# Softmax attention on one core: splitting the first V load, moving one transpose, and recutting the last V load

## The chip, the cores and the metric

The kernel runs on one core of a Trainium2 chip. The metric is the device time of one execution in microseconds. A core has a matrix engine (TensorE, PE in the profile, with weight loads listed apart as PEld), a vector engine (VectorE, DVE), a scalar engine (ScalarE, ACT), GpSimd (POOL), and SyncE (SP), which in this kernel only issues DMA transfers. Sixteen DMA engines move data between the chip's memory and the core's on-chip memory.

## The reference

Attention without a mask, for 8 x 16 = 128 heads, each with 16 queries, 2048 keys and values, and a head width of 256, all in bf16:

```python
B, H, Sq, Skv, Dh = 8, 16, 16, 2048, 256
scores = jnp.einsum('bhqd,bhkd->bhqk', q, k) * scale      # scale = Dh ** -0.5
attn   = softmax(scores, axis=-1)
out    = jnp.einsum('bhqk,bhkd->bhqd', attn, v)
```

K and V are 134 MB each and every byte of them is used once; Q and the output are 1 MB each.

## The kernel before

Eight heads form a block, so there are G = 16 blocks, and the last has the number 15. In a block, 8 heads x 16 queries fill the 128 partitions. K of a block comes in two units (e = 0 and 1) of 4 MB; a unit holds 128 partitions x 64 tokens x 256 values (T = 64). V of a block is 128 partitions x 128 tokens x 256 values, 8 MB.

On-chip there are four slots of 4 MB in the tensor SL, numbered VA, VB, KA and KB. V of a block fills VA and VB, the two K units of a block fill KA and KB. Only K of block 0 is an exception: it is loaded into VA and VB, so that K of block 1 can be loaded into KA and KB at once.

What a block goes through:

- VectorE transposes K in place, in two halves (h = 0 and 1) per unit: the helper kt(e, h, slot), line 195. Each transpose counts up c_kt.
- TensorE multiplies K by the queries into four banks of S_ps (lines 309 and 310, called from qk; for block 0 from a loop of its own). It works unit by unit and half by half, each half waiting for its transpose. c_qk counts 4 per finished unit, so 8 per block.
- VectorE takes the maximum over S_ps (line 218), ScalarE the exponential into P_sb (line 292), VectorE transposes the weights into PTa and PTb (lines 229 and 231) and makes the reciprocal of the sum (line 234).
- ScalarE (line 277) and VectorE (lines 202 and 204) copy the weights into PTz, the layout that TensorE reads. Half of these copies must wait until TensorE has used up the weights of the block before.
- TensorE multiplies the weights by V in 128 steps, one per token (the function pv, line 331). It counts up c_pv once per 16 tokens, so 8 per block. c_pv starts at 8, so that the counts of block b reach 8 * b + 16 at its end.
- ScalarE scales the result by the reciprocal (line 271) and issues the store of the block's output.

TensorE's order is: scores of block 0; then for r = 1 to 16 the scores of block r (if there is one) and after them the V product of block r - 1. Before some V products a few spare matmuls into X_ps run (line 310 also); the rounds at both ends have none.

SyncE issues all loads, in the order of its program (on_sync, lines 128 to 156), all on one queue: Q, the two K units of block 0, the two of block 1, V of block 0; then for each further block its two K units and V of the block before. A load is preceded by a wait until its slot has been used up: a K unit of block j waits for c_qk (the scores of the same unit of block j - 1), V of a block waits for c_pv (the V product of the block before). V of block 0 goes into VA and VB, where K of block 0 was, and so waits for c_qk 8: the scores of both units of block 0. The last two V loads (blocks 14 and 15) are cut into pieces by tokens (PIECES, lines 104 and 105); a piece starts when the product of the block before has passed its tokens, and the product of its own block waits for each piece, on a semaphore for every piece but the first.

VectorE's program (on_vector) before its loop over blocks transposes the four halves of K of block 0 and the first half of the first unit of block 1, line 213. Inside the loop, behind the maximum, a branch taken in block 0 alone transposes the second half of that unit (line 222), and another one, behind the reciprocal, both halves of the second unit (line 238).

All orders are written out by hand; there is no scheduler. The functions:

Of the kernel before, what the change touches and what calls it, by code (L numbers as in the profile page):

```python
# [14 lines left out]
T = 64  # L15
SPARE = 5
VA, VB, KA, KB = 0, 1, 2, 3
C = 16


def bass_standalone__softmax_full_bidir__sampling_kernel(
# [11 lines left out]
    last = G - 1  # L33
# [5 lines left out]
    vb = v.rearrange("b h s d -> (b h s) d").rearrange("(g p t) d -> g p t d", p=128, t=2 * T)  # L39
# [3 lines left out]
    with ExitStack() as es:  # L43
# [22 lines left out]
        def sem(name):  # L66
            return ec(nc.semaphore(name))
# [3 lines left out]
        s_k = [sem("s_ka"), sem("s_kb")]  # L71
        s_kl = [sem("s_kla"), sem("s_klb")]
        s_v = sem("s_v")
        s_st = sem("s_st")
        s_fin = sem("s_fin")
        c_pool = sem("c_pool")
# [4 lines left out]
        c_qk = sem("c_qk")  # L81
# [8 lines left out]
        c_pv = sem("c_pv")  # L90
# [11 lines left out]


        PIECES = {last - 1: [(0, 56), (56, 40), (96, 32)],
                  last: [(0, 37), (37, 27), (64, 19), (83, 14), (97, 10), (107, 7), (114, 5), (119, 4), (123, 3), (126, 2)]}

        s_p = {w: {a: sem("s_p%d_%d" % (w, a)) for a, n in PIECES[w][1:]} for w in PIECES}
        VW = SL[:, VA:VB + 1, :, :].rearrange("p a t d -> p (a t) d")


        def weights(e, r, x):
            rows = slice(32 * r, 32 * r + (32 if x else 16))
            m = 32 * r + 16 * x
            if e == x:
                src = PTa[rows, :, 16 * x:16 * x + 16]
            else:
                src = PTb[rows, e:e + T, 16 * x:16 * x + 16]
            return PTz[rows, e, :, m:m + 16], src, mk[rows, :]

        def qx(Q, a):  # L120

            return (QTu[32 * a:32 * a + 32, 8 * Q:8 * Q + 8, :, :].rearrange("p u c y -> p c u y"),
                    QXu[32 * Q:32 * Q + 32, a, :, :, :].rearrange("p u c y -> p c u y"))

        def load_k(eng, g, e, slot, t0, n, s):
            eng.dma_start(SL[:, slot, t0:t0 + n, :], ku[2 * g + e, :, t0:t0 + n, :]).then_inc(s, 16)

        def on_sync(eng):
            def load_v(w, a, n):

                if isinstance(w, int) and w == 0:
                    eng.wait_ge(c_qk, 8)
                else:
                    eng.wait_ge(c_pv, 8 * w + (a + n + C - 1) // C)
                eng.dma_start(VW[:, a:a + n, :], vb[w, :, a:a + n, :]).then_inc(s_p[w][a] if a else s_v, 16)  # L135

            eng.dma_start(QX, qh).then_inc(s_q, 16)  # L137
            for g, s0, s in ((0, VA, s_k0), (1, KA, s_k)):
                for e in range(2):
                    load_k(eng, g, e, s0 + e, 0, T, s[e])  # L140
            load_v(0, 0, 2 * T)
            with nc.Fori(2, last, engines=[SP]) as j:
                for e in range(2):
                    eng.wait_ge(c_qk, 8 * j + 4 * e - 4)
                    load_k(eng, j, e, KA + e, 0, T, s_k[e])
                load_v(j - 1, 0, 2 * T)
            for e in range(2):
                eng.wait_ge(c_qk, 8 * last + 4 * e - 4)
                load_k(eng, last, e, KA + e, 0, T // 2, s_k[e])
                load_k(eng, last, e, KA + e, T // 2, T // 2, s_kl[e])  # L150
            for w in PIECES:
                for a, n in PIECES[w]:
                    load_v(w, a, n)
            eng.wait_ge(c_ev, G + 1)
            eng.dma_start(oh[last], O_fin[:]).then_inc(s_fin, 16)
            eng.wait_ge(s_fin, 16)
# [19 lines left out]
        def on_vector(eng):  # L176
            eng.memset(QW[:].rearrange("p e m x -> p (e m x)").bitcast(F32), 0.0).then_inc(c_qt, 1)
            eng.memset(mk[:], 1.0).then_inc(c_mk, 1)
            eng.memset(P_sb[:, 0:16], 0.0).then_inc(c_mk, 1)
            eng.memset(P_sb[:, 2064:2080], 0.0).then_inc(c_mk, 1)  # L180
            eng.wait_ge(c_mk, 3)
            for r in range(4):
                eng.memset(mk[32 * r:32 * r + 16, :], 0.0).then_inc(c_mk, 1)
            eng.wait_ge(s_q, 16)
            qf = QX.bitcast(F32)
            eng.transpose(qf, qf).then_inc(c_qt, 1)  # L186
            eng.wait_ge(c_qt, 2)
            for a in range(4):
                eng.tensor_copy(*qx(0, a)).then_inc(c_qt, 1)
            fa = PTa[:].rearrange("p t x -> p (t x)")  # L190
            fb = PTb[:].rearrange("p t x -> p (t x)")

            def kt(e, h, slot):
                x = SLf[:, slot, 32 * h:32 * h + 32, :].rearrange("p t i -> p (t i)")
                eng.transpose(x, x).then_inc(c_kt, 1)  # L195

            def copies(e, rs):
                for r in rs:
                    for x in range(2):
                        dst, src, m = weights(e, r, x)  # L200
                        if x:
                            ins = eng.tensor_scalar(out=dst, in0=src, scalar1=m, scalar2=None, op0=ALU.mult)  # L202
                        else:
                            ins = eng.tensor_copy(dst, src)  # L204
                        ins.then_inc(c_cd, 1)

            for e in range(2):
                eng.wait_ge(s_k0[e], 16)
                for h in range(2):
                    kt(e, h, VA + e)  # L210

            eng.wait_ge(s_k[0], 16)
            kt(0, 0, KA)
            eng.wait_ge(c_pool, 2)
            eng.wait_ge(c_mk, 7)
            with nc.Fori(0, G, engines=[DVE]) as g:  # L216
                eng.wait_ge(c_qk, 8 * g + 8)
                eng.tensor_reduce(out=negm[:], in_=S_ps[:].rearrange("p c n -> p (c n)"),  # L218
                                  axis=AX.X, op=ALU.max, negate=True).then_inc(c_mx, 1)
                gg = eng.to_reg(g)  # L220
                with eng.If_eq(gg, 0):
                    kt(0, 1, KA)
                for h in range(2):
                    eng.wait_ge(c_ex[h], g + 1)
                    if h == 0:

                        eng.wait_ge(c_cp, 10 * g + 1)
                    n = 1024 + 32 * h
                    eng.transpose(fa[:, 1024 * h:1024 * h + 1024],  # L229
                                  P_sb[:, 16 + 1024 * h:16 + 1024 * h + 1024]).then_inc(c_pt, 1)  # L230
                    eng.transpose(fb[:, 1024 * h:1024 * h + n], P_sb[:, 1024 * h:1024 * h + n]).then_inc(c_pt, 1)  # L231
                eng.tensor_reduce(out=ltot[:], in_=lsum[:], axis=AX.X, op=ALU.add).then_inc(c_ri, 1)
                eng.wait_ge(c_ri, 2 * g + 3)
                eng.reciprocal(rinv[:, bass.ds(g + 2, 1)], ltot[:]).then_inc(c_ri, 1)
                with eng.If_eq(gg, 0):
                    eng.wait_ge(s_k[1], 16)
                    for h in range(2):
                        kt(1, h, KB)

                mid = eng.to_reg(((g + 15) & 16) + ((g + 1) & 16))  # L240
                with eng.If_eq(mid, 16):
                    eng.wait_ge(s_k[0], 16 * g + 16)
                    kt(0, 0, KA)
                eng.wait_ge(c_pv, 8 * g + 4)
                copies(0, (2, 3))
                with eng.If_eq(mid, 16):
                    eng.wait_ge(s_kl[0], ((g + 2) & 16) + 1)
                    kt(0, 1, KA)
                eng.wait_ge(c_pv, 8 * g + 8)
                copies(1, (3,))  # L250
                with eng.If_eq(mid, 16):
                    eng.wait_ge(s_k[1], 16 * g + 16)
                    kt(1, 0, KB)
                    eng.wait_ge(s_kl[1], ((g + 2) & 16) + 1)
                    kt(1, 1, KB)
# [49 lines left out]
        def on_tensor(eng):  # L305
# [16 lines left out]
            def pv(lim):  # L322

                for t in range(2 * T):
                    if t == T:
                        eng.wait_ge(c_cp, 10 * r + 1)
                        eng.wait_ge(c_cd, 6 * r)
                    for w in s_p:
                        if t in s_p[w]:
                            eng.wait_ge(s_p[w][t], lim[w])  # L330
                    ins = eng.matmul(O_ps[:, 0:D], PTz[:, t // T, t % T, :], VW[:, t, :],  # L331
                                     start=(t == 0), stop=(t == 2 * T - 1))
                    if t % C == C - 1:
                        ins.then_inc(c_pv, 1)
# [18 lines left out]
            with nc.Fori(1, G + 1, engines=[PE]) as r:  # L353
# [20 lines left out]
                pv(lim)  # L374

        on_sync(nc.sync)
        on_gpsimd(nc.gpsimd)
        on_vector(nc.vector)
# [30 lines left out]
```

## Time and profile before

| what | value |
|---|---|
| median of 3 runs | 635.7 us (635.33, 635.70, 636.56) |
| the profiled execution | 636.47 us, span 635.2 us |
| mean granted clock of TensorE | 0.976 |
| TensorE matmul busy | 536.8 us, 85% |
| VectorE busy | 444.2 us, 70% |
| ScalarE busy | 241.8 us, 38% |
| read from memory | 269.48 MB |
| mean rate over the span | 426 GB/s |
| K unit transposes (line 195) | 64, 4434 ns each |
| V product steps (line 331) | 2048, 274 ns each, overlapping |

The span runs from the first to the last recorded instruction or transfer; the execution's time is a little longer. Times in the profile count from the start of the span, in us. PE, PEld, DVE, ACT and POOL are the engines named above; a q behind an engine's name is its instruction queue. L195 is line 195 of the kernel. A row of the chain gives start, length and what the time went to. A row of a timeline gives start, length, engine, line, operation, destination and source, the count, and in square brackets how long the engine had been idle before and what ended that. A row of windows gives the stretch, its length, the busy time of PE, PEld, DVE, ACT and POOL with the number of instructions, the granted TensorE clock (1.00 is full speed), the busy share of the DMA engines and the rate in GB/s; in it a DMA record is counted where it starts, with its whole length, so that short windows can show shares above 1.

### The profile page before, as it was taken

Reading aid. Unit: us, or ns where it says so; the run is one execution under the profiler, and the core shown is the slowest. Engines: PE = TensorE matmul, PEld = TensorE weight load, DVE = VectorE, ACT = ScalarE, POOL = GpSimd, SP = SyncE. Lnnn points to the kernel's source line nnn. Section 1 sums busy time; section 2 is a strip of 40 time slices with the busy share of each in tenths; the row PEclk is TensorE's granted clock in tenths of the full one; section 3 lists DMA queues with packets and bytes.
Section 4 is the critical chain, followed back from the end, with each engine's and each line's share of the span. In section 5 each row is a group of like instructions: output and inputs, shape, how many; then the busy total and the mean of one; then the engine's idle time right before and its main releaser. Section 6 shows DMA issues by size and latency. Waiting matters only on the chain.

```text
span 635.2 us, 8052 instructions
## 1 busy us (share of the span) xinstructions
PE 536.8 (85%) x3271; PEld 274.5 (43%) x2561; DVE 444.2 (70%) x285; ACT 241.8 (38%) x309; POOL 21.5 (3%) x18
## 2 busy tenths in 40 slices
PE   1658979899798898978989789898888988889988
PEld 0112724517244182542725336263352724518377
DVE  5979795766948658496575966759567594769740
ACT  1025542623426233352424425244262342623552
POOL 7600000000000000000000000000000000000000
PEclk9998999999999998999989999898999989999999
DMA  8999999999999999999999999999999999999997
GB/s 365 450 435 400 427 435 427 434 424 431 459 404 457 406 440 440 426 451 416 448 430 420 445 417 444 449 407 458 405 457 412 428 442 431 451 406 429 429 423 280
DMA packets 11234, 270.56 MB, mean 426 GB/s; under 512 B 1248, under 2 KB 3552, under 8 KB 4192
## 3 DMA queue, kind: packets, MB, share of 16 engines
q1 hardware_dynamic: 9072, 269.55, 98.6%
q10 hardware_dynamic: 2160, 0.98, 0.5%
q8 instruction: 1, 0.02, 0.0%
q14 instruction: 1, 0.01, 0.0%
HBM read 269.48 MB, written 1.05 MB: 426 GB/s over the span
## 4 chain that ended last, share of the span: by engine, by line
DMA 53%; PE 37%; DVE 5%; issue 4%; SPq 0%; DVEq 0%; ACT 0%
DMA SL<-in_v_dram 48%; PE O_ps L331 32%; DMA SL<-in_k_dram 5%; DVE SL L195 4%; PE S_ps L309 3%; PE S_ps L310 2%; DVE PTa L229 0%; DVE PTb L231 0%; DVE PTz L202 0%; DVE PTz L204 0%; SPq L135 0%; ACT O_fin L271 0%; SPq L137 0%; DVEq L240 0%; DVEq L216 0%
## 5 line engine op out<-in xcount | busy, mean ns | idle before, releaser
L195 DVE STREAM_TRANSPOSE SL<-SL 128x4096 f32<-128x4096 f32 x64 | 282.4, 4434 | 80.5 <-DMA SL<-in_k_dram 79.7
L309 PE MATMUL S_ps<-SL,QW 128*128 128x512 bf16 (+1 forms) x512 | 206.2, 403 | 70.4 <-DVE SL L195 60.9
L331 PEld LDWEIGHTS O_ps<-SL,PTz 128*128 128x128 bf16 x2048 | 200.1, 98 | 102.2 <-DMA SL<-in_v_dram 77.6
L331 PE MATMUL O_ps<-SL,PTz 128*128 128x256 bf16 x2048 | 228.0, 274 | 12.6 <-DMA SL<-in_v_dram 12.6
L310 PE MATMUL S_ps<-SL,QW 128*128 128x512 bf16 (+1 forms) x512 | 204.7, 400 | 0.0
L309 PEld LDWEIGHTS S_ps<-SL,QW 128*128 128x128 bf16 (+1 forms) x512 | 74.3, 145 | 246.3 <-issue 154.4
L263 ACT ACTIVATE QW<-QT 32x256 bf16 x64 | 26.9, 420 | 201.8 <-PE S_ps L310 200.7
L218 DVE TENSOR_REDUCE negm<-S_ps 128x1 f32<-128x2048 f32 x16 | 36.7, 2292 | 58.8 <-PE S_ps L310 58.8
L277 ACT ACTIVATE PTz<-PTa 16x1024 bf16<-16x1024 bf16 x32 | 33.8, 1056 | 114.4 <-PE O_ps L331 99.7
L310 PE MATMUL X_ps<-QT,QW 128*128 128x512 bf16 x195 | 52.7, 379 | 3.4
L277 ACT ACTIVATE PTz<-PTb 16x1024 bf16<-16x1024 bf16 x48 | 50.6, 1055 | 10.9 <-ACT O_fin L271 10.1
L277 ACT ACTIVATE PTz<-PTa,mk 32x1024 bf16<-32x1024 bf16 x48 | 54.3, 1130 | 0.0
L229 DVE STREAM_TRANSPOSE PTa<-P_sb 128x1024 bf16<-128x1024 bf16 x32 | 39.1, 1222 | 20.5 <-ACT P_sb L292 20.5
L231 DVE STREAM_TRANSPOSE PTb<-P_sb 128x1024 bf16<-128x1024 bf16 (+1 forms) x32 | 39.0, 1218 | 0.0
L292 ACT ACTIVATE P_sb<-S_ps,negm 128x1024 bf16<-128x1024 f32 x32 | 35.3, 1109 | 5.4 <-DVE negm L218 5.4
L277 ACT ACTIVATE PTz<-PTb,mk 32x1024 bf16<-32x1024 bf16 x32 | 36.2, 1132 | 0.0
L271 ACT ACTIVATE O_fin<-O_ps,rinv 128x256 bf16<-128x256 f32 x16 | 7.6, 474 | 52.5 <-PE O_ps L331 52.5
L202 DVE TENSOR_SCALAR PTz<-PTb,mk 32x1024 bf16<-32x1024 bf16 x32 | 15.2, 476 | 0.0
L204 DVE COPY PTz<-PTa 16x1024 bf16<-16x1024 bf16 x32 | 13.5, 422 | 1.6 <-PE O_ps L331 0.6
L169 POOL COPY QT<-PTz 32x1024 bf16<-32x1024 bf16 x12 | 14.3, 1193 | 3.1 <-DVE PTz L186 2.4
L204 DVE COPY PTz<-PTb 16x1024 bf16<-16x1024 bf16 x16 | 6.8, 424 | 3.4 <-PE O_ps L331 3.0
L309 PE MATMUL S_ps<-PTz 128*128 128x512 bf16 x1 | 0.6, 609 | 9.8 <-ACT QW L263 9.8
(21 smaller groups left out, 38.8 us busy)
## 6 DMA issues: line engine op xcount, KB each, us to landing
SL<-in_k_dram SPq DMA_DIRECT2D x30, 4096.0 KB, 24.3
SL<-in_k_dram SPq DMA_DIRECT2D x4, 2048.0 KB, 22.0
SL<-in_v_dram SPq DMA_DIRECT2D x1, 3584.0 KB, 21.0
SL<-in_v_dram SPq DMA_DIRECT2D x1, 2560.0 KB, 23.6
SL<-in_v_dram SPq DMA_DIRECT2D x1, 2368.0 KB, 10.6
SL<-in_v_dram SPq DMA_DIRECT2D x1, 2048.0 KB, 25.0
SL<-in_v_dram SPq DMA_DIRECT2D x1, 1728.0 KB, 13.1
SL<-in_v_dram SPq DMA_DIRECT2D x1, 1216.0 KB, 12.6
```

Source lines behind the costliest of these rows:

```text
L195: eng.transpose(x, x).then_inc(c_kt, 1)
L202: ins = eng.tensor_scalar(out=dst, in0=src, scalar1=m, scalar2=None, op0=ALU.mult)
L204: ins = eng.tensor_copy(dst, src)
L218: eng.tensor_reduce(out=negm[:], in_=S_ps[:].rearrange("p c n -> p (c n)"), axis=AX.X, op=ALU.max, negate=True).then_inc(c_mx, 1)
L229: eng.transpose(fa[:, 1024 * h:1024 * h + 1024], P_sb[:, 16 + 1024 * h:16 + 1024 * h + 1024]).then_inc(c_pt, 1)
L231: eng.transpose(fb[:, 1024 * h:1024 * h + n], P_sb[:, 1024 * h:1024 * h + n]).then_inc(c_pt, 1)
L263: eng.activation(dv, src(a), ACTF.Copy, scale=scale).then_inc(c_qw, 1)
L277: eng.activation(dst, src, ACTF.Copy, scale=m if x else 1.0).then_inc(c_cp, 1)
L292: eng.activation(P_sb[:, 16 + 1024 * h:16 + 1024 * h + 1024], sv, ACTF.Exp, bias=negm[:], scale=1.0, accum_out=lsum[:, h:h + 1]).then_inc( ...
L309: return eng.matmul(dst, w, x, start=start, stop=stop, skip_group_check=not check)
L310: return eng.add_instruction(mybir.InstMatmult(name=nc.get_next_instruction_name(), engine=PE, start_tensor_calc=start, stop_tensor_calc=stop,
L331: ins = eng.matmul(O_ps[:, 0:D], PTz[:, t // T, t % T, :], VW[:, t, :], start=(t == 0), stop=(t == 2 * T - 1))
```

## The change

Three edits, in three places.

1. V of block 0 is loaded in two halves of 64 tokens. The first half goes into VA and waits only for the first unit's scores of block 0 (c_qk 4); the second goes into VB and waits for c_qk 8 as before. The second half has a semaphore of its own, s_v0, and the V product waits for it at token 64 (in every block; after block 0 it is passed already).
2. Both halves of the first unit of block 1 are transposed ahead of VectorE's loop. The branch behind the maximum is gone.
3. V of the last block comes in nine pieces of 30, 25, 20, 16, 12, 10, 7, 5 and 3 tokens instead of ten of 37, 27, 19, 14, 10, 7, 5, 4, 3 and 2.

```diff
+        s_v0 = sem("s_v0")
...
-                  last: [(0, 37), (37, 27), (64, 19), (83, 14), (97, 10), (107, 7), (114, 5), (119, 4), (123, 3), (126, 2)]}
+                  last: [(0, 30), (30, 25), (55, 20), (75, 16), (91, 12), (103, 10), (113, 7), (120, 5), (125, 3)]}
...
             def load_v(w, a, n):
-                if isinstance(w, int) and w == 0:
-                    eng.wait_ge(c_qk, 8)
-                else:
-                    eng.wait_ge(c_pv, 8 * w + (a + n + C - 1) // C)
+                eng.wait_ge(c_pv, 8 * w + (a + n + C - 1) // C)
                 eng.dma_start(VW[:, a:a + n, :], vb[w, :, a:a + n, :]).then_inc(s_p[w][a] if a else s_v, 16)
...
-            load_v(0, 0, 2 * T)
+            for e in range(2):
+                eng.wait_ge(c_qk, 4 * e + 4)
+                eng.dma_start(VW[:, T * e:T * e + T, :], vb[0, :, T * e:T * e + T, :]).then_inc(s_v0 if e else s_v, 16)
...
             eng.wait_ge(s_k[0], 16)
-            kt(0, 0, KA)
+            for h in range(2):
+                kt(0, h, KA)
             eng.wait_ge(c_pool, 2)
             eng.wait_ge(c_mk, 7)
             with nc.Fori(0, G, engines=[DVE]) as g:
...
                 gg = eng.to_reg(g)
-                with eng.If_eq(gg, 0):
-                    kt(0, 1, KA)
...
                 for t in range(2 * T):
                     if t == T:
+                        eng.wait_ge(s_v0, 16)
                         eng.wait_ge(c_cp, 10 * r + 1)
                         eng.wait_ge(c_cd, 6 * r)
```

## The prediction

> **What bounds the kernel now.** I read the page first (busy shares, slices, the chain by engine), then the chain in order of time, the windows of one long stretch, SP's own queue, and last the two places that the change touches: the first 85 us and the last 35.
>
> The page: busy share of the DMA engines in forty slices, and the chain that ended last, by line.
>
> ```profile
> DMA  8999999999999999999999999999999999999997
> ...
> DMA SL<-in_v_dram 48%; PE O_ps L331 32%; DMA SL<-in_k_dram 5%; DVE SL L195 4%; PE S_ps L309 3%; PE S_ps L310 2%; DVE PTa L229 0%; DVE PTb L231 0%; DVE PTz L202 0%; DVE PTz L204 0%; SPq L135 0%; ACT O_fin L271 0%; SPq L137 0%; DVEq L240 0%; DVEq L216 0%
> ```
>
> The chain in order of time (start, length, what), and the window over eleven blocks (length, busy by engine, clock, DMA share, GB/s).
>
> ```profile
> 67.07 13.99 PE O_ps L331 x128
> 81.22 24.06 DMA SL<-in_v_dram
> 105.33 14.16 PE O_ps L331 x128
> 119.65 24.53 DMA SL<-in_v_dram
> ```
>
> ```profile
> 105.33:533.44 428.11, 375.79 (x2278) 188.06 (x1761) 300.27 (x189) 164.18 (x209) 0.00 (x0) 0.97 1.00 433
> ```
>
> The chain looks like a ring of V load and V product, but 24.5 us are more than 8 MB need: at 433 GB/s 8.39 MB take 19.4 us, so the V load stands about 5 us in line behind K. With a DMA share of 1.00 over 428 us the stream of loads sets the pace. Only what shortens the stream, or what lies before its first byte and after its last, changes the time.
>
> **Part 1: V of block 0 in two loads.** SP's queue, two rows of DVE that end when a K unit lands, the end of the first unit's product on the chain, and the landing of V of block 0 (us after its issue):
>
> ```profile
> 1.19 2.08 SPq L126 DMA_DIRECT2D SL<-in_k_dram  x4
> 42.99 0.33 SPq L135 DMA_DIRECT2D SL<-in_v_dram  x1
> 56.79 10.80 SPq L126 DMA_DIRECT2D SL<-in_k_dram  x2
> ```
>
> ```profile
> 25.10 8.77 DVE L195 STREAM_TRANSPOSE SL<-SL 128x4096 f32<-128x4096 f32 x2 [0.94 <-DMA SL<-in_k_dram]
> ...
> 34.81 4.45 DVE L195 STREAM_TRANSPOSE SL<-SL 128x4096 f32<-128x4096 f32 x1 [0.94 <-DMA SL<-in_k_dram]
> ```
>
> ```profile
> 25.46 0.22 PE S_ps L310
> ```
>
> ```profile
> SL<-in_v_dram SPq DMA_DIRECT2D x1, 22.1
> ```
>
> The four K loads are issued together and land 34.81 - 25.10 = 9.71 us apart, so the fourth lands near 44.5. V of block 0 is issued only at 42.99, 1.5 us before that, and lands at 42.99 + 22.1 = 65.1. That is 20.6 us after the fourth K unit, where two units' worth takes 2 x 9.71 = 19.4. So 1.2 us are lost. The fine windows (records counted where they start; last columns DMA share and GB/s) show where:
>
> ```profile
> 42.50:42.75 0.25, 0.25 (x3) 0.00 (x0) 0.00 (x0) 0.00 (x0) 0.00 (x0) 1.00 4.25 1835
> 43.75:44.00 0.25, 0.00 (x0) 0.00 (x0) 0.25 (x1) 0.25 (x1) 0.00 (x0) 1.00 0.84 262
> 44.00:44.25 0.25, 0.00 (x0) 0.00 (x0) 0.25 (x1) 0.23 (x2) 0.00 (x0) 1.00 8.86 2884
> ```
>
> ```profile
> 44.00:45.00 1.00, 0.00 (x0) 0.00 (x0) 1.00 (x1) 0.92 (x3) 0.00 (x0) 1.00 2.97 983
> 49.00:50.00 1.00, 1.00 (x4) 0.27 (x2) 1.00 (x2) 0.00 (x0) 0.00 (x0) 0.50 2.27 983
> ```
>
> The last K packets start at 42.6 and take 4.25 x 0.25 x 16 / 14 = 1.21 us (14 of 32 KB), so they end at 43.8; the bulk of V's first packets starts about 44.15, a gap of 0.35. In 44 to 45 start 15 packets of 64 KB (983 GB/s x 1 us) with 2.97 x 16 / 15 = 3.17 us each, in 49 to 50 fifteen with 2.42: another 0.75. Together 1.1, against 1.2 by the landings. I take 1.15.
>
> After the change the first 64 tokens need only the first unit's product (c_qk 4), done at 25.68, when SP has nothing else to do. The load joins the line behind two K units, as each K unit of the start did, and the second 64 tokens are issued at 42.99 with 9.7 us of V ahead of them. K of block 2, next on SP, waits for c_qk 12 at 56.79, after both. So the 1.15 us should go; price of the second load: 0.33 us of SP's idle time. The packets become 32 KB instead of 64, and 2 x 1.21 is 2.42: nothing.
>
> Bounds: nothing, if the second load pays a start of its own; at the other end 2.4, since V of block 0 to V of block 1 is 105.28 - 65.1 = 40.2 us where the next blocks take 119.65 + 24.53 - 105.28 = 38.9, and those 1.3 could be an after-effect of the same start. A loss has no place: the bytes are the same and are asked for no later.
>
> [...]
>
> The new wait (s_v0, at token 64 of every V product) stands where two waits stand already. Behind it queue the second 64 matmuls, and ACT's and DVE's copies and SP's V loads wait for those. In block 0 the second half lands near 63.9, and PE gets to token 64 at about 72 (below). Later it is passed already; at most one matmul's pace, 14.16 / 128 = 0.11 us, inside the 5 us for which a V load stands in line: nothing.
>
> **Part 2: the transpose moved ahead of the maximum.**
>
> ```profile
> 43.00 2.29 DVE L218 TENSOR_REDUCE negm<-S_ps 128x1 f32<-128x2048 f32 x1 [3.74 <-PE S_ps L310]
> 45.21 4.43 DVE L195 STREAM_TRANSPOSE SL<-SL 128x4096 f32<-128x4096 f32 x1
> ...
> 54.37 0.17 DVE L234 RECIPROCAL rinv<-ltot 128x1 f32 x1 [0.16 <-DVE ltot L232]
> 54.49 8.77 DVE L195 STREAM_TRANSPOSE SL<-SL 128x4096 f32<-128x4096 f32 x2
> ...
> 67.11 2.29 DVE L218 TENSOR_REDUCE negm<-S_ps 128x1 f32<-128x2048 f32 x1 [1.40 <-PE S_ps L310]
> ...
> 75.61 0.16 DVE L234 RECIPROCAL rinv<-ltot 128x1 f32 x1
> ```
>
> DVE idles 3.74 us before the first maximum. The moved transpose runs 39.3 to 43.7, so the maximum starts 0.7 late. ACT's exponentials and the first unit's product of block 1 move with it: that product, whose end releases K of block 2, ends at 57.5 instead of 56.8, still 6 us before V of block 0 has landed. Cost: nothing. From maximum to reciprocal without a transpose between takes 75.61 - 67.11 = 8.5 us (block 1), so block 0's reciprocal starts at 52.2 instead of 54.37, and the two transposes of the second unit, the score product and the V product behind them come 2.1 us earlier: V product about 65.0 to 79.1 instead of 67.07 to 81.22. V of block 1 is then issued at 79.1.
>
> This saves nothing by itself, but it guards part 1. With the stream 1.15 us earlier, the last K unit of block 2 lands near 63.9 + 19.4 = 83.3. Issued at 81.22, V of block 1 would have a lead of 2.1 us, between 1.5 (cost 1.15 us in block 0) and the present 84.5 - 81.22 = 3.3. At 79.1 the lead is 4.2. If this cover were gone, up to 1.15 would return. The block dropped from DVE's loop runs beside the stream: nothing.
>
> **Part 3: the last V in nine pieces.** The chain, the V issues (first and last start), the landing of the last piece after its issue, and four windows:
>
> ```profile
> 606.60 10.59 DMA SL<-in_v_dram
> 617.19 0.04 issue
> 617.23 15.83 PE O_ps L331 x128
> ```
>
> ```profile
> L135 SPq DMA_DIRECT2D SL<-in_v_dram x27: 327/333/436, 43.0 to 617.1; - x27
> ```
>
> ```profile
> SL<-in_v_dram SPq DMA_DIRECT2D x1, 128.0 KB, 14.4
> ```
>
> ```profile
> 85.28:88.69 3.41, 1.70 (x8) 0.67 (x5) 3.35 (x4) 3.39 (x4) 0.00 (x0) 1.00 1.30 561
> 88.69:92.10 3.41, 2.06 (x10) 0.49 (x4) 3.41 (x1) 0.17 (x1) 0.00 (x0) 1.00 0.85 368
> 614.35:617.76 3.41, 1.48 (x14) 1.08 (x13) 0.83 (x2) 1.50 (x3) 0.00 (x0) 1.00 0.99 421
> 617.76:621.18 3.42, 3.42 (x18) 2.45 (x17) 0.00 (x0) 3.37 (x5) 0.00 (x0) 0.50 0.99 414
> ```
>
> Here PE, not the stream, ends last. The last piece lands at 617.1 + 14.4 = 631.5, but the product runs 15.83 us from 617.23, to 633.06, where others take 14.16, because the granted clock was 0.50 from 617.76 on for 3.42 us. PE had been busy for 1.48 of the 3.41 us before (0.43); a window with 1.70 of 3.41 (0.50) was followed by the full clock.
>
> A token is 65.5 KB, 0.151 us at 433 GB/s. With 30 tokens instead of 37 the first piece lands 7 x 0.151 = 1.06 earlier, at 616.13 on the old time line; it is also issued earlier (32 tokens of the product before, not 48), so nothing holds it. PE then idles some 0.9 us instead of 1.9 and should keep its clock: 616.13 + 14.16 = 630.3, ahead of the stream. With the half clock all the same it would be 616.13 + 15.83 = 631.96. The last piece lands at 631.5 less about 0.06 for one piece fewer (91 tokens after the first piece are 13.8 us, landings 14.3 apart, 0.5 over nine pieces). Three matmuls, 2 x 0.11 + 0.27, give an end near 632.0 either way. Gain 633.06 - 632.0 = 1.05. Bounds: nothing, or a loss of 0.5 (half clock late, below), to 1.3.
>
> **Sum.** The profiled execution took 636.47 us, of which 635.2 are the span and 1.27 lie around it. 636.47 - 1.15 - 0 - 1.05 = 634.3. The runs shown are 635.33, 635.70 and 636.56. The half clock at the end is part of the profiled execution; without it that one comes to 635.4, near the lower two. Against the median of 635.7 the gain is 1.4 us, 0.22%, just over the 0.2% (1.3 us, a bound at 634.4) that a measurement of this kernel can tell from no change.
>
> **The rivals.** (a) The start cost only moves: the second load, or V of block 1, pays the 1.15. For it: every start with a short lead in the trace was paid. Against it: the lead is 9.7 us, and queued K loads pay nothing. 635.4.
>
> (b) Slower than before: the half clock falls into the end of the last product. Nine pieces let PE run ahead and wait at each; if its busy share falls to 0.43 within some 3.41 us, the next such stretch runs at half speed with no slack. The last 3.4 us hold 22 tokens at 0.151, which at 0.22 each take 4.9 instead of 3.4: 1.5 us, so 635.8, above the median. Against it: PE's share there is 0.11 / 0.151 = 0.73, far above 0.43. [...]
>
> (c) The 1.3 us lost between V of block 0 and V of block 1 are an after-effect of the late start and go too: 633.0. No view shows their cause.
>
> **Chances.** Forecast 0.60 (its own range 633.9 to 634.8), (a) 0.15, (b) 0.12, (c) 0.08, and 0.05 for a disturbance that I have no row for, slower. The range 633.7 to 635.6 takes in the forecast and (a) and leaves out (b) and (c). About 0.7 of the forecast lies under 634.4, so faster is 0.7 x 0.60 + 0.08 = 0.50; slower by over 0.2% (above 637.0) 0.07; within 0.43.
>
> **What would show it.** Right: first V issue near 25.7, no window around 44 without DMA records longer than a packet, V product of block 0 near 65.0 and V of block 1 issued near 79, landing near 104.1; at the end PE waits for pieces, at clock 1.00, and the product starts within 1 us of the end of the one before. Wrong: long packets where the second load or V of block 1 begins, a V of block 1 landing at 105.3 still, or a 0.50 clock in the last 10 us.

## The result and the profile after

The changed kernel takes 634.58 us (median of 22 runs, 634.24 to 634.72) against 635.72 us of the kernel before (22 runs, 635.06 to 636.73). The ratio is 0.9981, with a 95% interval from 0.9974 to 0.9988: 0.19% faster, between 0.12% and 0.26%. The forecast was 634.3, range 633.7 to 635.6. The profiled execution took 634.58 us, span 633.3, against 636.47 and 635.2. The spread shrank as well: 22 values lie within 0.48 us, where those of before are spread over 1.67 and six of 22 are above 636.2.

The chain of the changed kernel in order of time (start, length, what), first around the V loads of blocks 0 and 1, then at the end:

```profile
64.53 13.99 PE O_ps L332 x128
78.68 25.52 DMA SL<-in_v_dram
104.24 14.16 PE O_ps L332 x128
118.57 24.55 DMA SL<-in_v_dram
```

```profile
600.32 13.99 PE O_ps L332 x128
614.30 0.02 issue
614.32 13.88 DMA SL<-in_v_dram
628.20 0.05 issue
628.25 2.93 PE O_ps L332 x25
```

The V product of block 1 starts at 104.24 instead of 105.33: the stream is 1.09 us ahead. The product of block 15 ends at 628.25 + 2.93 = 631.18 instead of 633.06, which is 1.88 ahead, so 0.79 more came at the end. 1.88 is the whole difference of the two profiled executions (636.47 - 634.58 = 1.89).

The first step shows in SP's queue, in the landing of the second half of V of block 0 (us after its issue, the row of the stretch 40 to 50), and in the windows (records counted where they start; last columns DMA share and GB/s):

```profile
31.14 12.03 SPq L142 DMA_DIRECT2D SL<-in_v_dram  x2
57.33 7.72 SPq L127 DMA_DIRECT2D SL<-in_k_dram  x2
78.68 0.33 SPq L133 DMA_DIRECT2D SL<-in_v_dram  x1
```

```profile
SL<-in_v_dram SPq DMA_DIRECT2D x1, 4096.0 KB, 20.9
```

```profile
43.50:43.75 0.25, 0.00 (x0) 0.00 (x0) 0.25 (x1) 0.23 (x2) 0.00 (x0) 1.00 1.53 655
43.75:44.00 0.25, 0.00 (x0) 0.00 (x0) 0.25 (x1) 0.23 (x2) 0.00 (x0) 1.00 3.36 1442
49.00:50.00 1.00, 1.00 (x4) 0.16 (x1) 1.00 (x2) 0.00 (x0) 0.00 (x0) 0.50 1.21 524
```

The first half is issued at 31.14, the second at 31.14 + 12.03 - 0.33 = 42.84, and it lands at 63.7; before, V of block 0 landed at 65.1. The first 16 packets of V start between 43.5 and 44.0 (5 and 11 of 32 KB) and take (1.53 + 3.36) x 0.25 x 16 / 16 = 1.22 us each, as the 1.21 in 49 to 50. The last 16 packets of K start between 42.25 and 42.75 (5 and 11 as well) and also take 1.22 us, so V's begin where they end. The gap (0.35 us before) and the long first packets (3.17 us of 64 KB before) are gone.

The second step, VectorE's timeline:

```profile
34.68 8.77 DVE L196 STREAM_TRANSPOSE SL<-SL 128x4096 f32<-128x4096 f32 x2 [0.95 <-DMA SL<-in_k_dram]
43.38 2.25 DVE L220 TENSOR_REDUCE negm<-S_ps 128x1 f32<-128x2048 f32 x1
...
51.85 0.16 DVE L234 RECIPROCAL rinv<-ltot 128x1 f32 x1 [0.15 <-DVE ltot L232]
51.97 8.77 DVE L196 STREAM_TRANSPOSE SL<-SL 128x4096 f32<-128x4096 f32 x2
```

Both halves run back to back, the maximum comes 0.4 late, the reciprocal 2.5 early, and the V product of block 0 ends 2.5 us earlier, at 78.5 to 78.7.

The third step, TensorE's product of block 15, first before, then in the changed kernel with the ScalarE and VectorE rows ahead of it, and the window over the last 24 us:

```profile
617.23 15.81 PE L331 MATMUL O_ps<-SL,PTz 128*128 128x256 bf16 x128 [1.93 <-DMA SL<-in_v_dram]
```

```profile
614.58 0.47 ACT L271 ACTIVATE O_fin<-O_ps,rinv 128x256 bf16<-128x256 f32 x1 [1.58 <-PE O_ps L332]
614.67 0.48 DVE L203 TENSOR_SCALAR PTz<-PTa,mk 32x1024 bf16<-32x1024 bf16 x1
615.37 3.45 PE L332 MATMUL O_ps<-SL,PTz 128*128 128x256 bf16 x30 [1.08 <-DVE PTz L203]
619.04 2.90 PE L332 MATMUL O_ps<-SL,PTz 128*128 128x256 bf16 x25 [0.22 <-DMA SL<-in_v_dram]
622.29 8.88 PE L332 MATMUL O_ps<-SL,PTz 128*128 128x256 bf16 x73 [0.34 <-DMA SL<-in_v_dram]
```

```profile
608.00:632.00 24.00, 21.27 (x186) 17.16 (x184) 3.33 (x9) 11.41 (x12) 0.00 (x0) 1.00 0.87 362
```

TensorE idles 1.08 us ahead of the product instead of 1.93, and the clock stays at 1.00. Only before does the profile put this wait down to the first piece of V.

### The profile page after: what moved, and what is told of

Same layout as the page of the kernel before. It is cut to its first block, busy times and chain, and to the rows that moved or that the text cites. A ratio compares the mean times of both kernels' runs of the same rounds, so it can differ in the third digit from the quotient of the medians.

```text
span 633.3 us, 8100 instructions
## 1 busy us (share of the span) xinstructions
PE 539.7 (85%) x3336; PEld 272.9 (43%) x2561; DVE 444.2 (70%) x285; ACT 241.8 (38%) x309; POOL 21.5 (3%) x18
## 3 DMA queue, kind: packets, MB, share of 16 engines
HBM read 269.48 MB, written 1.05 MB: 427 GB/s over the span
## 4 chain that ended last, share of the span: by engine, by line
DMA 57%; PE 34%; DVE 5%; issue 3%; SPq 0%; DVEq 0%; ACT 0%
DMA SL<-in_v_dram 49%; PE O_ps L332 32%; DMA SL<-in_k_dram 8%; DVE SL L196 4%; PE S_ps L309 1%; PE S_ps L310 1%; DVE PTb L231 0%; DVE negm L220 0%; DVE PTa L229 0%; DVE PTz L203 0%; DVE PTz L205 0%; SPq L133 0%; SPq L127 0%; ACT O_fin L271 0%; SPq L135 0%
## 5 line engine op out<-in xcount | busy, mean ns | idle before, releaser
L310 PE MATMUL X_ps<-QT,QW 128*128 128x512 bf16 x260 | 58.2, 379 | 0.0
## 6 DMA issues: line engine op xcount, KB each, us to landing
SL<-in_v_dram SPq DMA_DIRECT2D x1, 1920.0 KB, 11.3
```

The lines of the kernel that those rows point to most:

```text
L310: return eng.add_instruction(mybir.InstMatmult(name=nc.get_next_instruction_name(), engine=PE, start_tensor_calc=start, stop_tensor_calc=stop,
```

## The experiments

Two things had to be told apart: which part gives the stream its 1.1 us, and whether the rest is the half clock in the last product. Unless another base is named, the edits are to the kernel before.

**The split alone,** with its semaphore s_v0 and the wait at token 64 as in the change.

```diff
+            for e in range(2):
+                eng.wait_ge(c_qk, 4 * e + 4)
+                eng.dma_start(VW[:, T * e:T * e + T, :], vb[0, :, T * e:T * e + T, :]).then_inc(s_v0 if e else s_v, 16)
-            load_v(0, 0, 2 * T)
```

> Part 1 alone: V of block 0 in two loads, the transpose and the ten pieces as before. If the early first load is what shortens the stream and V of block 1, still issued near 81.2, is early enough: V of block 1 lands near 104.2 instead of 105.28 and the median falls by 1.0, to about 634.7, with some executions near 635.5 where the half clock meets the last product. If the earlier V product of part 2 is needed as a guard: V of block 1 pays a start cost of its own, lands between 104.6 and 105.3, and the median falls by 0 to 0.6.

Median 635.6 (634.47 to 636.45, 12 runs), ratio 0.9997 (0.9988 to 1.0005). The profiled execution took 634.83. In it and in the two further traces below, V of block 1 lands at 104.5 (81.16 + 23.3), 104.6 and 104.7: between 105.3 and the 104.1 to 104.3 of the four traces with all of parts 1 and 2. So the guard is needed, but its worth is 0.2 to 0.6 us of the 1.1, not all of it. The median says less than it seems, as the next two runs show.

**The split alone, two more traces.** The same kernel.

> The split alone once more, for its trace. Its executions fell into groups near 634.5, 635.6 and 636.2. If the group depends on whether the late issue of V of block 1 meets the slowest DMA engine: an execution above 635.3 shows V of block 1 landing at 105 or later, with pauses or long packets in its first microseconds on that engine too; one below 634.9 shows it landing near 104.6. If it depends on the half clock in the last product alone: V of block 1 lands at 104.6 in both.

> As the run before it: a third trace of the split alone, with the same two readings.

635.80 and 635.97 us. The chain's last product, in the first trace (634.83 us):

```profile
616.61 14.82 PE O_ps L333 x128
```

in the second (635.80 us), with a window of it:

```profile
616.57 15.83 PE O_ps L333 x128
```

```profile
617.00:620.00 3.00, 3.00 (x16) 2.14 (x15) 0.00 (x0) 2.98 (x4) 0.00 (x0) 0.50 0.97 407
```

and in the third (635.97 us):

```profile
616.74 15.83 PE O_ps L333 x128
```

In the third the chain also shows V of block 1, issue and time to landing:

```profile
81.03 23.69 DMA SL<-in_v_dram
```

V of block 1 lands within 0.25 us in all three, and the last products start within 0.2; the last product takes 1.01 us more in the two slower ones. From 617 to 620 the clock was 1.00 in the first trace, 0.50 in the second and 0.66 in the third, which had 0.77 from 620 to 623: 1.7 us lost in all, as by 3.4 us at 0.50. That accounts for 635.80 - 634.83 = 0.97, since the product starts 0.04 earlier in the second trace than in the first. What sorts these three executions is the half clock, not the landing of V of block 1. That one DMA engine is slower than the others, as the expectation has it, no run shows. The values above 636.1 have no trace, and what they have besides is left open. It follows that the median of a kernel with ten pieces depends on how many of its executions happen to meet it; the landings in the traces are the better measure of the stream.

**The transpose alone.** Part 2's edit.

> Part 2 alone: the moved transpose with everything else as before. If the stream sets the pace: V product of block 0 ends near 78.9 instead of 81.22, V of block 1 is issued there and still lands at 105.3, median 635.7, no change. If the ring of V load and V product sets the pace instead: V of block 1 lands 2 us earlier and the median falls by about 2.

Median 635.4 (635.11 to 636.49), ratio 1.0001 (0.9992 to 1.0009).

```profile
65.33 14.16 PE O_ps L330 x128
79.65 25.41 DMA SL<-in_v_dram
105.11 4.98 PE O_ps L330 x44
```

V of block 1 is issued 1.6 us earlier and waits 1.4 us longer: the stream sets the pace. By itself the transpose buys 0.2 us at the most.

**The nine pieces alone.** Part 3's edit.

> Part 3 alone: nine pieces from 30 to 3, everything else as before. If the gain is that the last product no longer meets the half clock: the executions above 636 vanish, the values draw together around 635.4, the fastest stay where the fastest of before are (635.1 to 635.3), and no clock of 0.50 stands in the last 20 us. If the recut itself ends the stream earlier: the fastest value falls too, by 0.5 or more.

Median 635.71 (635.32 to 636.09), ratio 1.0000 (0.9991 to 1.0009). The range has closed from both sides: of the 35 runs of before beside it ten are above 636 and 16 below 635.4, of these eleven one (636.09) and two. The nine pieces take away the executions above 636 and make the quick ones a little slower. The traces say the same. From the landing of V of block 1 to the end of the last product pass 527.8 us in the three traces with ten pieces and the half clock, 526.8 to 526.9 in the five with ten pieces and the full clock, and 526.9 to 527.0 in the six with nine.

**Both other parts, with the ten pieces.** Edit to the changed kernel.

```diff
-                  last: [(0, 30), (30, 25), (55, 20), (75, 16), (91, 12), (103, 10), (113, 7), (120, 5), (125, 3)]}
+                  last: [(0, 37), (37, 27), (64, 19), (83, 14), (97, 10), (107, 7), (114, 5), (119, 4), (123, 3), (126, 2)]}
```

> Parts 1 and 2 with the ten pieces of before. If the gain of the two is the start cost alone: every value 1.0 below the like value of before, 634.1 to 635.7, median near 634.7, with the spread of before (over 1 us) since the last product can still meet the half clock. If nine pieces are what gives the gain: no better than before, 635.7.

Median 634.55 (634.16 to 635.42), ratio 0.9986 (0.9977 to 0.9995). Nine of eleven values lie between 634.16 and 634.73, two at 635.4. The two parts give the whole gain of the median without the recut. The profiled execution kept its clock (1.00 from 608 to 632):

```profile
79.32 24.82 DMA SL<-in_v_dram
```

```profile
616.24 14.80 PE L332 MATMUL O_ps<-SL,PTz 128*128 128x256 bf16 x128 [1.92 <-DMA SL<-in_v_dram]
```

It ends at 631.04, where the nine pieces' last row in the same view ends at 622.29 + 8.88 = 631.17, 0.13 later, though it starts 0.9 later. Of the 0.13, 0.06 is an earlier landing of V of block 1 (104.14 instead of 104.20).

**Two loads, both late.** Edit to the changed kernel.

```diff
-                eng.wait_ge(c_qk, 4 * e + 4)
+                eng.wait_ge(c_qk, 8)
```

> The changed kernel with both loads of V of block 0 waiting for c_qk 8: split, but not early. If the early issue is what counts: the first load starts with the short lead of before and pays for it, V of block 1 lands near 105.2, and the values go up by about 1.0 against the changed kernel, to 635.6. If two loads instead of one are what counts: as the changed kernel, 634.6. If each further load costs of itself: above 636.

Median 635.44 (635.09 to 636.12), ratio 0.9994 (0.9985 to 1.0003).

```profile
78.80 26.25 DMA SL<-in_v_dram
105.10 4.98 PE O_ps L332 x44
```

The 0.86 us against the changed kernel are back. Not the number of loads counts but the time of the first.

**A dose: V of block 0 cut at token 2 and at token 8.** Edit to the changed kernel (8 likewise).

```diff
+                a, b = ((0, 2), (2, 2 * T))[e]
+                eng.dma_start(VW[:, a:b, :], vb[0, :, a:b, :]).then_inc(s_v0 if e else s_v, 16)
-                eng.dma_start(VW[:, T * e:T * e + T, :], vb[0, :, T * e:T * e + T, :]).then_inc(s_v0 if e else s_v, 16)
...
-                    if t == T:
+                    if t == 2:
                         eng.wait_ge(s_v0, 16)
+                    if t == T:
```

> The changed kernel with V of block 0 cut at token 2 instead of 64: only 0.3 us of V stand ahead of the second load, so that at its issue the line holds some 1.8 us of work instead of 11. If a lead of 1.5 us costs 1.0 us and the cost falls with the lead: 635.2 to 635.6. If any load in the line ahead does: 634.6.

> The changed kernel with V of block 0 cut at token 8: 1.2 us of V ahead, a lead of about 2.7 us at the issue of the second load. If the start cost is the time from issue to a full stream, about 1.5 plus 1.1 = 2.6 us: nothing is left of it, 634.6 to 634.8. If a start needs more than 3 us: between 634.9 and 635.6.

Token 2: median 635.37 (634.79 to 637.74; the one value of 637.74 has no trace and stays unexplained). Token 8: 634.78 (634.37 to 635.66). V of block 1, issue and time to landing, cut at 2:

```profile
79.15 25.69 DMA SL<-in_v_dram
```

and cut at 8:

```profile
79.34 25.40 DMA SL<-in_v_dram
```

With leads of about 1.5, 1.8, 2.7 and 11 us, V of block 1 lands at 105.05 (both late), 104.84, 104.74 and 104.20, and the medians are 635.44, 635.37, 634.78 and 634.58. The cost falls with the lead; at 2.7 us 0.2 of it (by the medians) to 0.5 (by one trace each) is left, a little more than expected. Between 1.8 and 2.7 the landings differ by 0.1 only, no more than those of one kernel do.

At the landing of the load itself the same cost is larger and clearer. The table takes V loads of 8 MB with different leads. The lead is the time from the issue of V to the landing of the K unit ahead of it; where part of V is in line already (the two cuts and the last row), that part is added. A landing is the issue plus the time to landing.

| load | lead, us | lands after the K unit, us |
|---|---|---|
| V of block 0 in the kernel before | 1.5 | 20.6 |
| V of block 0 cut at token 2 | 1.8 | 20.5 |
| V of block 0 cut at token 8 | 2.7 | 20.4 |
| V of block 1 in the split alone, three traces | 3.3 to 3.5 | 19.9 to 20.2 |
| V of block 1 in the kernel before | 4.5 | 19.5 |
| V of block 0 in the changed kernel | 11 | 19.4 |

So 2.7 us of lead still cost about 1.0 us at this load. Some 0.5 of it comes back at the first K unit behind it, which lands 10.6 us later, against 11.1 to 11.2 in the four traces with all of parts 1 and 2. Why is open.

**Spare matmuls ahead of the last product.** TensorE's wait for the first piece is filled.

```diff
+                with eng.If_eq(rr, G):
+                    for _ in range(9):
+                        mm(X_ps[:], QT[:, 0:128], QT[:, 0:512], True, True, _ == 0, False)
                 lim = {last - 1: eng.to_reg(((r + 1) & 16) + 1), last: eng.to_reg((r & 16) + 1)}
```

> The kernel before, with nine spare matmuls into X_ps on TensorE between the products of blocks 14 and 15, some 1.9 us that fill its wait for the first piece. If TensorE's idling ahead of the last product is what halves the clock in some executions: no value above 636, all within 634.9 to 635.7, and the product of block 15 takes about 14.7 us at full clock. If the slow executions have another cause: the same share of about 3 in 10 above 636.

Median 635.46 (635.26 to 635.69, 11 runs), ratio 0.9991 (0.9982 to 1.0000). Twelve of the 33 runs of before beside it are above 636; of these eleven none is.

```profile
615.36 1.89 PE L310 MATMUL X_ps<-QT 128*128 128x512 bf16 x8
...
617.24 14.81 PE L331 MATMUL O_ps<-SL,PTz 128*128 128x256 bf16 x128
```

So the idling is what lets the clock fall here: with the wait filled, the clock of the profiled execution was 1.00 from 608 to 632, and the product took 14.81 us instead of 15.81. In the clock records of the kernel before, the half clock stands nine times, for 3.41 us each time (3.42 in the window of the last product). It begins at 47.73, 126.24, 204.75 and 242.29 us and so on, each time 78.51, 37.55 or 102.40 us after the time before, which are 23, 11 and 30 times 3.41 to within 0.1. An idle time of 1.92 to 1.96 us ahead of the same product brought it in three of six traces (the kernel before and two of the split alone; not the first of the split alone, the transpose alone or both with ten pieces). In the 3.41 us up to the product TensorE was thus busy for about (3.41 - 1.95) / 3.41 = 0.43 in all six, so that this share alone, from which the forecast's rival (b) starts, does not bring the half clock. What does is not shown.

**Ten pieces with spare matmuls, on top of parts 1 and 2,** and the changed kernel again on the same chip.

> Parts 1 and 2 with the ten pieces of before and nine spare matmuls between the last two products. If the half clock is all that is wrong with ten pieces: no value above 635, median 634.4 to 634.6, level with the changed kernel or 0.1 below it. If the nine pieces do something else besides: 0.2 or more above the changed kernel.

> The changed kernel once more, on the chip of the kernel with ten pieces and spare matmuls, to compare the two: 634.6, all values within 0.5.

634.47 (634.32 to 634.67) against 634.51 (634.20 to 634.76): level. Its last product:

```profile
616.16 14.80 PE L332 MATMUL O_ps<-SL,PTz 128*128 128x256 bf16 x128
```

It ends at 630.96, 0.2 before the changed kernel's 631.17. Recutting the pieces and filling the wait are two ways to the same thing, and no version here beats the changed kernel by more than runs differ.

## Why the prediction was right, and where not

The time lies 0.28 above the forecast, inside its range, and for the reasons given.

- **Part 1**, 1.15 forecast: 1.09 measured on the start of the product of block 1, 0.99 in the second trace of the changed kernel. It is measured with part 2, whose transpose alone moves that start by 0.2. The two causes, gap and long first packets, vanished together, and two late loads brought the cost back. One step was read wrongly: the first unit's product does not end at 25.68, a row in the middle of it, but lets the load go at 31.14. With K occupying the queue to about 44 this cost nothing.
- **A start of its own for the second load**, with which the forecast bounded the gain of part 1 at nothing, was not paid: the second half lands at 63.7, and 44.5 for the last K unit plus 19.4 is 63.9.
- **Part 2**, nothing by itself and a guard for part 1: right in kind (no change alone; the split without it gains less). The size was off: "up to 1.15 would return" was a bound, and 0.2 to 0.6 came back. The lead was misjudged as well. V of block 1 has 3.3 us there, not 2.1: the last K unit of block 2 lands at 84.5 (67.19 + 17.3), not 83.3, since the first one takes over a microsecond longer than the forecast had it. With that lead V lands 19.9 to 20.2 us after K instead of 19.4 to 19.5.
- **Part 3**, 1.05 forecast: 0.79 in the profiled pair. This is the mis-sized term. The forecast had the last piece land near 630.3 and the product end 0.5 us behind it, after three matmuls, at 632.0 - 1.15 = 630.85. The last piece landed near 630.5 (615.6 + 14.9), and the product ended 0.6 behind it. In place of the last piece the chain shows the piece of 10 tokens, which lands at 628.20, and behind it 25 tokens of product, 2.93 us, up to 631.18, without another wait: the three pieces after it land about as fast as TensorE takes their tokens, so it is not the last piece that it waits for.
- **The wait ahead of the last product** was forecast as 0.9 us, for the first piece, and was 1.08, not for the first piece. That piece landed at 615.1 (603.84 + 11.3), and TensorE began at 615.37, though elsewhere it starts 0.04 to 0.05 us after a landing that it waits for (617.19 and 617.23 before, 628.20 and 628.25 in the changed kernel). In all six traces with nine pieces the wait is 1.08. The profile names VectorE's copy (line 203), which by the code is needed only at token 64. What the code asks for at the start besides the piece is that ScalarE has taken the result of block 14 (c_ev), which ends at 615.05. That this is what ends the wait, and that a smaller first piece would gain nothing, was not tested.
- **Against the median** the forecast carried part 3 as a gain that only executions with the half clock have. It said so, but not what follows: against the median part 3 is worth nothing (nine pieces alone: ratio 1.0000), and the median gain is that of the stream, 1.14 us or 0.18%. That is just under the 0.2% that it was forecast to be just over.
- **Rival (a)**, the start cost only moves: false for the whole change, half true for the split alone. **Rival (b)**, the half clock late in the last product: nothing of it; the clock was 1.00 from 608 to 632, and of 22 values none is above 634.72. **Rival (c)**, that the 1.3 us between V of block 0 and V of block 1 are an after-effect of the late start: false. In the changed kernel V of block 0 starts without loss and lands at 63.7, and V of block 1 still lands 104.20 - 63.7 = 40.5 us later, against 40.2 before and 38.9 in the later blocks. The loss lies in the first K unit of block 2: it lands at 74.9 (57.33 + 17.6), 11.2 us after V of block 0, where the next one (64.72 + 20.0) takes 9.8 and V of block 1 behind it 19.5. What loses it stays open.

## What to carry to other kernels

Where a stream of loads sets the time, look for the load that is issued when the queue is nearly empty. Splitting off the part whose buffer is free earlier cost nothing here, but it can leave a later load with a short lead in its turn: 2.7 and 3.3 us of queued work were not enough, 4.5 nearly were (20.4, about 20 and 19.5 us from K's landing to V's, against 19.4 at 11 us), and here the moved transpose, which lets that load be issued earlier, supplied the lead. And when single executions differ by a whole microsecond, sort them by their traces before reading medians; 1.0 us of this kernel's spread of 1.67 was one stretch of 3.42 us at a clock of 0.50.

## What was not expected

If the values above 636 are taken for it, of which one was traced, the half clock in the last product struck about 3 in 10 executions of the kernel before (six of 22, ten of 35, twelve of 33, five of 21). It lengthened the product by 1.01 us, 15.83 against 14.82. Two kernels that differ by 0.2 to 0.6 us of stream could so show medians 1.05 us apart (635.6 for the split alone, 634.55 with the transpose): only four of the one's 14 executions lie below 635, but nine of the other's eleven. Why the split alone met the half clock so often is open.

A product that starts 0.9 us earlier on smaller pieces ended about 0.1 us later than one that started late and ran through. With the clock at 1.00 in both, the end of the nine pieces still hung on a landing (628.20, with 25 tokens to go), and their early start went into waits (0.22 and 0.34 us between the rows) and longer rows (15.23 us together, against 14.80).
